# A linear-attention recurrence fused with a gated feed-forward: u read in rows and turned on TensorE, and an order table that reaches one group further

## Chip, core and metric

One core of a Trainium2 chip runs the whole program. The metric is the device time of one execution in microseconds (us). Engines are called as the profile calls them: PE (TensorE), DVE (VectorE), ACT (ScalarE), POOL (GpSimd) and SP (SyncE, which issues almost all DMAs).

## The reference

```python
# r, k, v, w: (4, 8, 768, 48) = batch, heads, sequence, head size; u: (8, 48)
for t in range(S):
    cur = np.einsum('bhd,bhe->bhde', u[None] * kt, vt)
    y[:, :, t] = np.einsum('bhd,bhde->bhe', rt, state + cur)
    state = wt[:, :, :, None] * state + np.einsum('bhd,bhe->bhde', kt, vt)
# x: y as (3072 tokens, 384)
g = x @ w_gate                        # (384, 1536)
silu = g * (1.0 / (1.0 + np.exp(-g)))
out = (silu * (x @ w_val)) @ w_out    # (1536, 384)
```

Everything is float32.

## The kernel before

The sequence is cut into 24 chunks of 128 tokens (6 for each batch). Two heads share a tile, so a chunk has 4 pairs of heads on 112 partitions. One chunk n of the recurrence takes these steps, named as in the kernel:

- loads on SP: `ws` (decays), `kr` (k and r), `vt` (v) and, from chunk 6 on, `nat` (k and r with tokens on partitions);
- DVE: `scan`, `seed`, `scan2` (products of decays), `kq` and `re` (k and r scaled by them, in place), `pred` (one for each head of a pair: keeps the causal part), `sps` and `st` (the state), `ru`, `ruk` and `a0` (the u term from `nat`), and for later chunks `xl`;
- ACT: `whole`, `kn`, `diag`, `vz`, `spb`, `xh`, and `xl` for early chunks;
- PE: `kb` (k turned), `sc` (scores), `dl` (what a chunk adds to the state), `y` (output, already turned for the next matmul), `xm`.

For chunks 0 to 5 the u term comes another way: `prod` (DVE) makes k times r, and `kb` has four matmuls of `prod` with `u_head`, a tile that holds u with head size on partitions, two columns for each pair. `prod` has one buffer (it shares it with `nat`), so `prod:1` must wait until `kb:0` has read `prod:0`. `diag` needs the result through `kn`.

The feed-forward works on groups of 4, 2, 4, 4, 4, 4 and 2 chunks (`GROUPS`), in 12 blocks of 128 hidden columns each. A block f of group g is: `gv:g:f:0` and `gv:g:f:1` (gate and value, 9 matmuls each, on 512 tokens or 256 for a group of two), `silu` (ACT), `sg` (DVE), `hh` (ACT), `hl` (DVE), and `po` (3 matmuls for each chunk of the group). Weights are split in an upper and a lower part (`raw`, `top`, `low`, `shift`, `sign`, `plus`, `upper`, `lower`) while they come in, once, in group 0. The two `gv` results in PSUM have two buffers, so `gv` of the next block waits for `silu` and `sg` of this one. `spin:n` is n matmuls on a constant, for no result.

Two things set the order. The string `ORDER` (line 47) lists steps by name, and on each engine, SP included, the instructions run in that order, each waiting for what it needs. What stands behind the table is written as loops (from line 605): blocks of the remaining groups, with the steps of the remaining chunks (`attention_steps`) strewn between them, and here the framework's scheduler places DVE and ACT work, also among the last steps of the table. `FREE = 2` says that the table holds the blocks of groups 0 and 1; it holds chunks 0 to 9 whole, and the preparation of chunk 10.

`u_head` is filled at lines 182 to 188: a memset on DVE and two DMAs on ACT's queue, each of which reads four rows of 48 numbers and writes them across partitions, one number at a time.

Of the kernel before, what the change touches and what calls it, by code (L numbers as in the profile page):

```python
# [48 lines left out]
scan2:0 kb:0 spin:7 kn:0 re:0 ws:2 diag:0:0 prod:1 sc:0 spin:19 scan:1 diag:0:1 pred:0:0 whole:1
seed:1 kq:1 top:0 pred:0:1 scan2:1 dl:0 spin:6 low:0 st:0 ws:3 shift:0 kb:1 vz:1 vz:0 re:1 y:0  # L50
kn:1 sign:0 diag:1:0 sc:1 spin:9 kr:4 prod:2 vt:2 diag:1:1 plus:0 xh:0 pred:1:0 upper:0 raw:2 xm:0
spin:9 pred:1:1 xl:0 lower:0 top:1 dl:1 spin:16 sps:1 low:1 shift:1 st:1 sign:1 spb:1 y:1 spin:5
scan:2 plus:1 xh:1 vt:3 whole:2 kr:5 xm:1 spin:10 xl:1 seed:2 upper:1 raw:3 kq:2 sps:2 kb:2 spin:5
scan2:2 spb:2 vz:2 kn:2 lower:1 ws:4 diag:2:0 dl:2 spin:11 st:2 diag:2:1 re:2 prod:3 sc:2 spin:13
top:2 scan:3 vz:3 pred:2:0 whole:3 low:2 kq:3 seed:3 kb:3 pred:2:1 scan2:3 y:2 spin:5 kn:3
diag:3:0 shift:2 ws:5 re:3 vt:4 diag:3:1 sps:3 sc:3 sign:2 xh:2 low:3 xm:2 spin:9 pred:3:1
pred:3:0 xl:2 plus:2 spb:3 dl:3 top:3 y:3 spin:7 prod:4 raw:4 upper:2 scan:4 xh:3 vt:5 st:3 vz:4
xm:3 spin:5 whole:4 lower:2 xl:3 gv:0:0:0 kq:4 shift:3 seed:4 sign:3 kb:4 silu:0:0 gv:0:0:1 top:4
scan2:4 kn:4 plus:3 ws:6 vz:5 diag:4:0 gv:0:1:0 re:4 raw:5 upper:3 sg:0:0 scan:5 sc:4 hh:0:0
diag:4:1 lower:3 gv:0:1:1 whole:5 low:4 seed:5 shift:4 hl:0:0 sign:4 po:0:0 silu:0:1 top:5 sg:0:1  # L60
plus:4 low:5 gv:0:2:0 hh:0:1 sps:4 raw:6 pred:4:0 upper:4 pred:4:1 gv:0:2:1 spb:4 hl:0:1 lower:4
silu:0:2 dl:4 gv:0:3:0 sg:0:2 st:4 hh:0:2 shift:5 hl:0:2 gv:0:3:1 sign:5 top:6 low:6 sps:5 plus:5
po:0:1 silu:0:3 prod:5 upper:5 raw:7 sg:0:3 po:0:2 kq:5 hh:0:3 lower:5 hl:0:3 kb:5 gv:0:4:0
shift:6 kn:5 nat:6 diag:5:0 scan2:5 sign:6 po:0:3 ws:7 top:7 re:5 low:7 plus:6 y:4 silu:0:4 scan:6
upper:6 raw:8 gv:0:4:1 ru:6 diag:5:1 vt:6 seed:6 lower:6 kr:6 whole:6 spb:5 gv:0:5:0 xh:4 ruk:6
sg:0:4 a0:6 hh:0:4 shift:7 xm:4 nat:7 diag:6:0 gv:0:5:1 hl:0:4 sign:7 top:8 po:0:4 vz:6 plus:7
silu:0:5 xl:4 low:8 kq:6 raw:9 sc:5 sg:0:5 upper:7 scan2:6 gv:0:6:0 hh:0:5 lower:7 ws:8 gv:0:6:1
hl:0:5 shift:8 silu:0:6 re:6 sign:8 po:0:5 top:9 sg:0:6 low:9 plus:8 gv:0:7:0 hh:0:6 scan:7
upper:8 raw:10 gv:0:7:1 hl:0:6 whole:7 seed:7 silu:0:7 lower:8 po:0:6 pred:5:1 sg:0:7 shift:9
hh:0:7 pred:5:0 kb:6 gv:0:8:0 top:10 sign:9 kn:6 hl:0:7 low:10 y:5 plus:9 silu:0:8 ru:7 raw:11  # L70
upper:9 po:0:7 ruk:7 a0:7 diag:6:1 kr:7 lower:9 nat:8 vt:7 gv:0:8:1 diag:7:0 shift:10 xh:5 sign:10
xm:5 gv:0:9:0 xl:5 sg:0:8 plus:10 top:11 sc:6 hh:0:8 upper:10 kq:7 gv:0:9:1 pred:6:1 low:11 hl:0:8
pred:6:0 silu:0:9 po:0:8 lower:10 vz:7 sg:0:9 gv:0:10:0 shift:11 hh:0:9 ru:8 sign:11 gv:0:10:1
ruk:8 plus:11 dl:6 a0:8 upper:11 y:6 st:6 nat:9 hl:0:9 kb:7 lower:11 silu:0:10 vt:8 po:0:9 kr:8
diag:8:0 sg:0:10 kn:7 sps:7 scan2:7 hh:0:10 gv:0:11:0 diag:7:1 ru:9 ws:9 hl:0:10 vz:8 spb:7
gv:0:11:1 ruk:9 silu:0:11 re:7 a0:9 scan:8 nat:10 po:0:10 xh:6 sg:0:11 whole:8 seed:8 hh:0:11 kq:8
xm:6 hl:0:11 gv:1:0:0 xl:6 scan2:8 po:0:11 silu:1:0 ru:10 ws:10 re:8 ruk:10 sc:7 scan:9 ob:0:1
ob:0:0 out:0:1 gv:1:0:1 out:0:0 seed:9 whole:9 pred:7:1 pred:7:0 gv:1:1:0 sg:1:0 dl:7 hh:1:0
ob:0:3 y:7 hl:1:0 st:7 out:0:3 silu:1:1 sps:8 ob:0:2 out:0:2 po:1:0 diag:8:1 vt:9 kr:9 kb:8
diag:9:0 gv:1:1:1 a0:10 nat:11 gv:1:2:0 spb:8 sg:1:1 kn:8 hh:1:1 gv:1:2:1 vz:9 hl:1:1 xh:7  # L80
silu:1:2 po:1:1 sg:1:2 hh:1:2 kq:9 xm:7 gv:1:3:0 hl:1:2 xl:7 scan2:9 po:1:2 silu:1:3 re:9 ws:11
sc:8 scan:10 gv:1:3:1 pred:8:1 whole:10 seed:10 gv:1:4:0 pred:8:0 sg:1:3 dl:8 hh:1:3 y:8 hl:1:3
st:8 silu:1:4 sps:9 kb:9 diag:9:1 vt:10 po:1:3 kr:10 kn:9 gv:1:4:1 xh:8 spb:9 xm:8 gv:1:5:0 sg:1:4
xl:8 hh:1:4 vz:10 sc:9 hl:1:4 silu:1:5 gv:1:5:1 kq:10 pred:9:0 gv:1:6:0 sg:1:5 scan2:10 hh:1:5
dl:9 gv:1:6:1 st:9 check:10 re:10 po:1:4 hl:1:5 pred:9:1 silu:1:6 po:1:5 ws:12 sg:1:6 hh:1:6
gv:1:7:0 hl:1:6 gv:1:7:1 silu:1:7 y:9 sg:1:7 hh:1:7 hl:1:7 gv:1:8:0 xh:9 kr:11 vt:11 gv:1:8:1
silu:1:8 gv:1:9:0 sg:1:8 po:1:6 po:1:7 hh:1:8 hl:1:8 gv:1:9:1 silu:1:9 gv:1:10:0 sg:1:9 hh:1:9
gv:1:10:1 hl:1:9 silu:1:10 gv:1:11:0 sg:1:10 gv:1:11:1 po:1:8 po:1:9 hh:1:10 hl:1:10 xm:9
# [670 lines left out]
```

## Time and profile before

| | us |
|---|---|
| runs of this kernel, median of 3 (lowest, highest) | 593.75 (593.44, 595.37) |
| the profiled execution's own time | 594.61 |
| its span, first to last instruction | 592.9 |
| PE busy | 572.4 |
| DVE busy | 325.4 |
| ACT busy | 282.8 |

The difference of 1.7 between the profiled execution's time and its span lies ahead of the first instruction and behind the last. A busy PE in this profile is one with a matmul under way, and since matmuls overlap, their durations add up to more than the time. What a step costs PE is therefore read from where the next step begins. A wait is given as the idle time of an engine, with the engine or the DMA that ended it; the chain of waits follows the work that ended last back through the program.

### The profile page before, as it was taken

What the parts mean: (1) busy time and instruction counts of PE and PEld (TensorE: products, weight loads), DVE (VectorE), ACT (ScalarE), POOL (GpSimd) and SP (SyncE); (2) the same over time, 40 slices, a digit from 0 to 9 for tenths busy, and PEclk for the clock granted to TensorE, in tenths of its full rate; (3) what the DMA queues carried; (4) which work ended last, traced back from release to release, by engine and by line L of the source; (5) the groups of instructions that cost most, each with busy time, mean ns of one, the idle gap of its engine ahead of it and who ended that gap; (6) DMA issues with size and microseconds to landing.
All of it is one profiled execution on the core that took longest, in us unless ns stands there. A gap on an engine that the chain in (4) does not pass through costs nothing.

```text
span 592.9 us, 12527 instructions
## 1 busy us (share of the span) xinstructions
PE 572.4 (97%) x5330; PEld 495.1 (83%) x5330; DVE 325.4 (55%) x511; ACT 282.8 (48%) x638; POOL 1.8 (0%) x11
## 2 busy tenths in 40 slices
...
GB/s 252 258 173 184 113 242 180 153 87 128 101 68 65 33 83 72 50 54 72 85 104 103 50 104 116 101 57 72 17 45 47 54 1 1 1 1 1 53 1 33
DMA packets 22734, 50.63 MB, mean 85 GB/s; under 512 B 2992, under 2 KB 9264, under 8 KB 22672
## 3 DMA queue, kind: packets, MB, share of 16 engines
...
q10 hardware_dynamic: 416, 0.00, 0.0%
...
## 4 chain that ended last, share of the span: by engine, by line
PE 87%; ACT 5%; DMA 4%; DVE 2%; issue 1%; ACTq 0%; DVEq 0%
PE gv L522 49%; PE po L556 25%; PE y L422 5%; PE sc L366 4%; PE idle L589 1%; PE dl L390 1%; DMA kr<-in_kr_dram 1%; DMA nat<-in_nat_dram 1%; PE kb L342 1%; DMA u_head<-in_u_rows_dram 1%; ACT at L327 1%; PE kb L344 1%; ACT kn L352 1%; ACT w_h L234 0%; ACT raw L213 0%
## 5 line engine op out<-in xcount | busy, mean ns | idle before, releaser
L522 PE MATMUL gv<-xh,w_h 128*128 128x512 f32 (+1 forms) x504 | 184.1, 365 | 2.4 <-ACT sg L531 2.3
L522 PE MATMUL gv<-xl,w_h 128*128 128x512 f32 (+1 forms) x504 | 182.1, 361 | 0.0
L522 PE MATMUL gv<-xh,w_l 128*128 128x512 f32 (+1 forms) x504 | 181.8, 361 | 0.0
L534 DVE TENSOR_TENSOR sg<-sg,gv 128x512 f32<-128x512 f32 (+1 forms) x84 | 50.9, 606 | 145.2 <-PE gv L522 135.0
L522 PEld LDWEIGHTS gv<-xh,w_h 128*128 128x128 f32 x504 | 94.7, 188 | 18.6 <-ACT sg L531 3.3
L522 PEld LDWEIGHTS gv<-xl,w_h 128*128 128x128 f32 x504 | 94.8, 188 | 14.9
L522 PEld LDWEIGHTS gv<-xh,w_l 128*128 128x128 f32 x504 | 94.8, 188 | 12.8
L556 PE MATMUL po<-w_h,hh 128*128 128x384 f32 x288 | 100.7, 350 | 0.4 <-ACT hh L539 0.4
L556 PE MATMUL po<-w_h,hl 128*128 128x384 f32 x288 | 97.2, 338 | 1.7 <-DVE hl L544 1.7
L556 PE MATMUL po<-w_l,hh 128*128 128x384 f32 x288 | 96.9, 336 | 0.0
L539 ACT ACTIVATE hh<-sg 128x512 fp32r<-128x512 f32 (+1 forms) x84 | 47.8, 569 | 98.0 <-DVE sg L534 93.5
L531 ACT ACTIVATE sg<-gv 128x512 f32<-128x512 f32 (+1 forms) x84 | 44.6, 531 | 96.0 <-PE gv L522 89.4
L544 DVE TENSOR_TENSOR hl<-sg,hh 128x512 fp32r<-128x512 f32 (+1 forms) x84 | 51.6, 614 | 46.1 <-ACT hh L539 45.7
L556 PEld LDWEIGHTS po<-w_h,hh 128*128 128x128 f32 x288 | 54.0, 187 | 7.0 <-issue 4.3
L556 PEld LDWEIGHTS po<-w_h,hl 128*128 128x128 f32 x288 | 54.1, 188 | 3.6 <-DVE hl L544 2.6
L556 PEld LDWEIGHTS po<-w_l,hh 128*128 128x128 f32 x288 | 54.0, 188 | 0.0
L327 ACT ACTIVATE at<-ident,a 128x128 f32<-128x128 f32 x144 | 45.5, 390 | 1.1 <-PE y L422 0.9
L371 DVE COPY_PREDICATED at<-mask,sc 128x512 f32<-128x512 uint32 x48 | 33.0, 729 | 6.4 <-PE sc L366 6.3
L303 ACT ACTIVATE ws<-ws 112x517 f32<-112x517 f32 x24 | 15.3, 639 | 43.3 <-DVE et L292 28.1
L275 DVE TENSOR_TENSOR_SCAN qt<-ws,d1q 112x516 f32<-112x516 f32 x24 | 29.5, 1227 | 1.5 <-DMA ws<-in_wt_dram 1.4
L287 DVE TENSOR_TENSOR kr<-kr,qt 112x512 f32<-112x512 f32 x24 | 16.5, 687 | 24.6 <-DMA kr<-in_kr_dram 24.6
L366 PE MATMUL sc<-kr 48*64 48x128 f32 x768 | 28.6, 282 | 1.2 <-ACT kn L352 1.2
...
## 6 DMA issues: line engine op xcount, KB each, us to landing
kr<-in_kr_dram SPq DMA_DIRECT2D x24, 448.0 KB, 4.1
...
vt<-in_vn_dram SPq DMA_DIRECT2D x24, 192.0 KB, 3.7
out_dram<-ob SPq DMA_DIRECT2D x24, 192.0 KB, 1.9
u_bc<-in_u_dram SPq DMA_DIRECT2D x1, 192.0 KB, 6.7
```

What stands on the lines that cost most here:

```text
L275: keep(nc.vector.tensor_tensor_scan(_flat(qts[n])[:, ::-1], wss[n][:, 1:][:, ::-1], _flat(d1q)[:, ::-1], 0.0, ALU.mult, ALU.add))
L287: keep(nc.vector.tensor_tensor(k, k, qts[n][:, :, 1:], ALU.mult))
L327: keep(nc.scalar.activation(a[:, p, :], ident, AF.Copy, scale=d))
L366: pin(nc.tensor.matmul(scs[n][j][ms, p, :], krs[n][o, 0, p, ms], krs[n][o, 1, p, :], start=True, stop=True,))
L371: keep(nc.vector.copy_predicated(ats[n, j], mask4, scs[n][j]))
L422: pin(nc.tensor.matmul(ys[n][32 * q : 32 * q + 32, b // 4, :], lhs, rhs, start=start[q] == i, stop=stop[q] == i,))
L522: pin(nc.tensor.matmul(ps, a[:, f, j, q * P : (q + 1) * P], x[:, q, :], start=m == 0, stop=m == 3 * NK - 1,))
L531: keep(nc.scalar.activation(sgs[g, f], ps, AF.Silu))
L534: keep(nc.vector.tensor_tensor(sgs[g, f], sgs[g, f], gvs.pop((g, f, 1)), ALU.mult))
L539: keep(nc.scalar.activation(hhs[g, f], t, AF.Copy))
L544: keep(nc.vector.tensor_tensor(hls[g, f], t, hhs[g, f].bitcast(F32), ALU.subtract))
L556: pin(nc.tensor.matmul(pos[g][j], a[:, ts], x[:, f, 2, :], start=f == 0 and i == 0, stop=f == NF - 1 and i == 2,))
```

## The change

The DMAs of u now read rows into a tile `u_two` (8 partitions, one for each head; heads of the second half of a pair 64 columns on). A new step `uh` turns it on PE into PSUM, and ACT copies it to `u_head`, which now holds its two columns per pair with a stride. `FREE` becomes 3: the table has the blocks of group 2 as well, chunks 0 to 13 whole and the preparation of chunk 14; all of the table is written anew.

```diff
-FREE = 2
+FREE = 3
...
-spin:22 ws:0 kr:0 ws:1 kr:1 raw:0 vt:0 scan:0 vt:1 kr:2 ub:0 seed:0 whole:0 raw:1 prod:0 kq:0 kr:3
+spin:21 uh ws:0 kr:0 ws:1 kr:1 raw:0 vt:0 scan:0 vt:1 kr:2 ub:0 seed:0 whole:0 raw:1 prod:0 kq:0
...
+    u_two = mp.tile([H, PR], F32, tag="ob", name="u_two", bufs=2)
+    u_head = cpool.tile([PR, 2, NPR], F32, tag="u_head", name="u_head")
+    nc.vector.memset(u_two, 0.0)
+    for j in range(2):
+        nc.scalar.dma_start(u_two[NPR * j : NPR * j + NPR, 64 * j : 64 * j + D], u_rows[j:H:2, :])
+
     warm = cpool.tile([1, 1], F32, tag="warm", name="warm")
...
-    u_head = cpool.tile([PR, NPR, 2], F32, tag="u_head", name="u_head")
-    nc.vector.memset(u_head, 0.0)
-    for j in range(2):
-        nc.scalar.dma_start(
-            u_head[64 * j : 64 * j + D, :, j], u_rows[j:H:2, :].rearrange("p d -> d p"),
-            allow_slow_non_contiguous=True,
-        )
...
+    def uh():
+        turned = psA.tile([PR, 2, NPR], F32, tag="pa", name="u_turned")
+        pin(nc.tensor.transpose(_flat(turned), u_two, ident[:H, :H]))
+        keep(nc.scalar.activation(u_head, turned, AF.Copy))
...
-                    kbs[n][:, p, PR : PR + 2], prods[n][:, p, :], u_head[:, p, :], start=True, stop=True,
+                    kbs[n][:, p, PR : PR + 2], prods[n][:, p, :], u_head[:, :, p], start=True, stop=True,
```

The first place is PE's order at the start, the last spin ahead of `kb:0` and what follows. Before:

```order
L589 LDWEIGHTS mask
L589 MATMUL idle<-mask 128x256
L342 MATMUL kb_168<-ident,kr_138 128x112
L344 MATMUL kb_168<-u_head,prod_162 128x2
L342 MATMUL kb_168<-ident,kr_138 128x112
```

With the change:

```order
L608 LDWEIGHTS mask
L608 MATMUL idle<-mask 128x256
L323 MATMUL u_turned<-ident,u_two 112x8
L361 MATMUL kb_171<-ident,kr_141 128x112
L363 MATMUL kb_171<-u_head,prod_165 128x2
```

One matmul has come in ahead of `kb:0`, and DVE's first 23 instructions are the same but for the memset.

The second place is DVE's order in group 1, where `nat_11` is the tile of `nat:11`, `kr_9` that of `kr:9`, and `sg_1_2` that of block 2. Before:

```order
L534 TENSOR_TENSOR sg_1_1_1823<-sg_1_1_1823,gv_1_1_1_1856 128x256
L544 TENSOR_TENSOR hl_1_1_1898<-sg_1_1_1823,hh_1_1_1885 128x256
L312 TENSOR_TENSOR nat_11_1868<-nat_11_1868,u_bc_106 128x384
L534 TENSOR_TENSOR sg_1_2_1901<-sg_1_2_1901,gv_1_2_1_1887 128x256
L287 TENSOR_TENSOR kr_9_1844<-kr_9_1844,qt_9_1735 112x512
L315 TENSOR_TENSOR nat_11_1868<-nat_11_1868 128x384
L544 TENSOR_TENSOR hl_1_2_1924<-sg_1_2_1901,hh_1_2_1910 128x256
```

With the change:

```order
L553 TENSOR_TENSOR sg_1_1_1827<-sg_1_1_1827,gv_1_1_1_1851 128x256
L563 TENSOR_TENSOR hl_1_1_1896<-sg_1_1_1827,hh_1_1_1883 128x256
L553 TENSOR_TENSOR sg_1_2_1899<-sg_1_2_1899,gv_1_2_1_1885 128x256
L301 TENSOR_TENSOR kr_9_1844<-kr_9_1844,qt_9_1713 112x512
L306 SCALAR_TENSOR_TENSOR et_9_1929<-ws_9_1516,d1q_84 112x516
L563 TENSOR_TENSOR hl_1_2_1951<-sg_1_2_1899,hh_1_2_1913 128x256
L312 TENSOR_TENSOR kr_9_1844<-kr_9_1844,et_9_1929 112x512
L331 TENSOR_TENSOR nat_11_1868<-nat_11_1868,u_bc_107 128x384
```

The first use of `nat:11` has moved behind `sg` and `hl` of block 2, `kq:9`, `scan2:9` and `re:9`.

The third place is DVE's order where the table ends and the scheduler's own work begins; before, this was in group 1 (blocks 7 to 8, chunk 11):

```order
L544 TENSOR_TENSOR hl_1_7_2250<-sg_1_7_2216,hh_1_7_2248 128x256
L319 TENSOR_REDUCE a0_12_2781<-nat_12_2575 128x8
L287 TENSOR_TENSOR kr_11_2263<-kr_11_2263,qt_11_2453 112x512
L292 SCALAR_TENSOR_TENSOR et_11_2481<-ws_11_1938,d1e_87 112x516
L534 TENSOR_TENSOR sg_1_8_2277<-sg_1_8_2277,gv_1_8_1_2267 128x256
```

With the change it is in group 2 (blocks 7 to 8, chunk 15):

```order
L563 TENSOR_TENSOR hl_2_7_3129<-sg_2_7_3105,hh_2_7_3122 128x512
L301 TENSOR_TENSOR kr_15_3124<-kr_15_3124,qt_15_3356 112x512
L338 TENSOR_REDUCE a0_16_3710<-nat_16_3478 128x8
L306 SCALAR_TENSOR_TENSOR et_15_3384<-ws_15_2931,d1e_87 112x516
L465 TENSOR_TENSOR xl_3_2711<-y_13_3074,xh_3_2710 128x3x128
L312 TENSOR_TENSOR kr_15_3124<-kr_15_3124,et_15_3384 112x512
L289 SCALAR_TENSOR_TENSOR qt_16_3541<-ws_16_3107,d1q_84 112x516
L331 TENSOR_TENSOR nat_17_3712<-nat_17_3712,u_bc_107 128x384
L297 RECIPROCAL d1e_87<-qt_16_3541 112x4
L334 TENSOR_TENSOR nat_17_3712<-nat_17_3712 128x384
L553 TENSOR_TENSOR sg_2_8_3164<-sg_2_8_3164,gv_2_8_1_3154 128x512
```

Nine instructions of later chunks now stand in one piece between `hl` of block 7 and `sg` of block 8; in group 1, where they stood in part, they are gone.

## Rows read from the trace of the kernel before

**Rows 1.** The page: busy time of each engine, share of the span, instructions.

```profile
PE 572.4 (97%) x5330; PEld 495.1 (83%) x5330; DVE 325.4 (55%) x511; ACT 282.8 (48%) x638; POOL 1.8 (0%) x11
```

**Rows 2.** Waits of PE: who waited for whom: us in total, times, longest.

```profile
PE kb L344 <- DMA u_head<-in_u_rows_dram: 3.2, 1, 3.2
...
PE sc L366 <- ACT kn L352: 1.2, 3, 0.6
```

**Rows 3.** Stretches: length, busy PE, PEld, DVE, ACT, POOL, clock, DMA share, GB/s.

```profile
10.05:12.20 2.15, 2.12 (x12) 2.15 (x13) 0.00 (x0) 0.00 (x0) 0.00 (x0) 0.50 1.11 351
...
15.60:49.20 33.60, 32.00 (x597) 25.63 (x594) 32.88 (x45) 27.82 (x60) 0.00 (x0) 1.00 0.67 200
49.20:136.40 87.20, 85.99 (x686) 73.44 (x684) 82.00 (x107) 60.13 (x109) 0.00 (x0) 1.00 0.51 161
```

**Rows 4.** Timeline of the start: start, us, engine, what [idle before, releaser].

```profile
2.54 4.01 PE L589 MATMUL idle<-mask 128*128 128x256 bf16 x22 [2.54 <-POOL mask L160]
...
6.59 0.31 PE L342 MATMUL kb<-ident,kr 112*128 112x112 f32 x1
...
7.91 0.69 DVE L298 TENSOR_TENSOR kr<-kr,et 112x512 f32<-112x512 f32 x1
...
10.08 0.56 PE L344 MATMUL kb<-u_head,prod 112*128 112x2 f32 x2 [3.17 <-DMA u_head<-in_u_rows_dram]
...
12.28 0.69 DVE L309 TENSOR_TENSOR prod<-kr 112x512 f32<-112x512 f32 x1 [3.68 <-PE kb L344]
...
15.80 0.74 DVE L371 COPY_PREDICATED at<-mask,sc 128x512 f32<-128x512 uint32 x1 [1.69 <-PE sc L366]
```

**Rows 5.** DMA issues: what, queue, count, size, median us from issue to landing.

```profile
kr<-in_kr_dram SPq DMA_DIRECT2D x24, 448.0 KB, 4.1
...
out_dram<-ob SPq DMA_DIRECT2D x24, 192.0 KB, 1.9
```

**Rows 6.** The two u_head DMAs, then kr:1: issued from, to; us to landing.

```profile
L185 ACTq DMA_DIRECT2D u_head<-in_u_rows_dram x2: 431/444/457, 2.1 to 2.6; - x2
...
DMA to landing us min/median/max: 6.5/6.9/7.4
...
L259 SPq DMA_DIRECT2D kr<-in_kr_dram x1: 427/427/427, 2.2 to 2.2; - x1
...
DMA to landing us min/median/max: 6.6/6.6/6.6
```

**Rows 7.** Stretches of groups 1 and 2: gv (L522), po (L556), then all instructions.

```profile
136.40:192.73 56.33, 28.75 (x217) 26.59 (x218) 1.00 0.30 88
...
136.40:192.73 56.33, 15.55 (x79) 13.34 (x78) 1.00 0.30 88
...
192.73:283.00 90.27, 89.63 (x797) 76.24 (x797) 45.24 (x72) 36.77 (x91) 0.00 (x0) 1.00 0.20 60
```

**Rows 8.** Chain of waits, undisturbed pieces: start, us, engine, line, matmuls.

```profile
106.95 1.67 PE y L422 x56
...
139.76 1.03 PE sc L366 x32
...
498.23 4.12 PE gv L522 x18
...
551.66 1.05 PE po L556 x6
552.71 2.12 PE gv L522 x18
```

**Rows 9.** Timeline of DVE in group 1: its waits for transfers.

```profile
151.14 0.56 DVE L312 TENSOR_TENSOR nat<-nat,u_bc 128x384 f32<-128x384 f32 x1 [1.64 <-DMA nat<-in_nat_dram]
...
165.70 0.56 DVE L312 TENSOR_TENSOR nat<-nat,u_bc 128x384 f32<-128x384 f32 x1 [2.60 <-DMA nat<-in_nat_dram]
...
179.42 0.69 DVE L287 TENSOR_TENSOR kr<-kr,qt 112x512 f32<-112x512 f32 x1 [1.27 <-DMA kr<-in_kr_dram]
```

**Rows 10.** Groups by line: count, then busy us and mean ns of one.

```profile
L275 DVE TENSOR_TENSOR_SCAN qt<-ws,d1q 112x516 f32<-112x516 f32 x24 | 29.5, 1227 | 1.5 <-DMA ws<-in_wt_dram 1.4
```

More of the change, by code (lines that the diff above doesn't have):

```diff
@@ L47 @@
 ORDER = """
-spin:22 ws:0 kr:0 ws:1 kr:1 raw:0 vt:0 scan:0 vt:1 kr:2 ub:0 seed:0 whole:0 raw:1 prod:0 kq:0 kr:3
[L49 to L88, printed above, removed]
@@ L89 @@
-silu:1:11 po:1:10 xl:9 sg:1:11 hh:1:11 hl:1:11
+spin:21 uh ws:0 kr:0 ws:1 kr:1 raw:0 vt:0 scan:0 vt:1 kr:2 ub:0 seed:0 whole:0 raw:1 prod:0 kq:0
+kr:3 scan2:0 kb:0 spin:6 re:0 kn:0 ws:2 diag:0:0 prod:1 sc:0 spin:19 scan:1 diag:0:1 pred:0:0
+whole:1 seed:1 kq:1 top:0 pred:0:1 scan2:1 dl:0 spin:7 low:0 st:0 ws:3 shift:0 kb:1 vz:1 vz:0 re:1
+y:0 sign:0 kn:1 diag:1:0 sc:1 spin:11 vt:2 prod:2 kr:4 diag:1:1 plus:0 xh:0 pred:1:0 raw:2 upper:0
+xm:0 spin:9 pred:1:1 xl:0 sps:1 lower:0 top:1 dl:1 spin:10 spb:1 st:1 shift:1 low:1 y:1 spin:5
@@ new lines @@
+scan:2 sign:1 whole:2 xh:1 vt:3 vz:2 kr:5 xm:1 spin:7 sps:2 xl:1 kq:2 spb:2 plus:1 kb:2 spin:5
+seed:2 kn:2 raw:3 prod:3 upper:1 dl:2 spin:13 scan2:2 diag:2:1 st:2 ws:4 re:2 diag:2:0 lower:1
+sc:2 spin:18 top:2 scan:3 low:2 pred:2:0 kq:3 vz:3 seed:3 whole:3 kb:3 pred:2:1 scan2:3 y:2 spin:4
+kn:3 diag:3:0 shift:2 ws:5 re:3 vt:4 xh:2 sps:3 sc:3 diag:3:1 sign:2 xm:2 spin:8 spb:3 pred:3:0
+xl:2 pred:3:1 top:3 dl:3 plus:2 y:3 spin:12 low:3 st:3 raw:4 scan:4 upper:2 vt:5 prod:4 xh:3
+lower:2 vz:4 xm:3 spin:5 whole:4 xl:3 gv:0:0:0 kq:4 shift:3 seed:4 sign:3 gv:0:0:1 silu:0:0
```

49 lines of the change are left out of this document (48 added, 1 removed).

## Prediction, made before the change was run

> **What bounds the kernel now.** I read the page first: PE is busy for 572.4 us, 97% of the span [rows 1]. So it is PE's own work that sets the time, and a change can gain only where PE does something useless or slow, or waits. The stretches, next, tell where. Up to 49.2 us the four first chunks are worked through and the first block of group 0 has not begun; from 15.6 on DVE is busy for 32.9 of 33.6 us there, so DVE sets the pace of the start [rows 3]. From 49.2 to 136.4 PE has 86.0 of 87.2 and DVE 82.0 [rows 3]: both nearly full. Then the waits of PE name the longest one: `kb:0` for the DMA of u_head, 3.2 us [rows 2]. The timeline shows what it costs behind PE: `kb:0` begins at 6.59, stops for u_head until 10.08, and `prod:1` on DVE, which needs the buffer that `kb:0` reads, starts at 12.28 after 3.68 idle; the first `pred` starts at 15.80 after another 1.69, for `sc:0` [rows 4]. Part of that is the clock: in 10.05 to 12.20 the granted clock was 0.50, the lower of the two levels (1.2 GHz), after PE had stood still for those 3.2 us [rows 2, 3].
>
> The second place is group 1. Undisturbed, nine `gv` matmuls on 256 tokens take 1.06 (2.12 for 18), six `po` matmuls 1.05, `sc` 1.03, `y` 1.67 [rows 8]. The stretch from 136.4 to 192.73 holds 24 `gv` stages (217 matmuls, one of them the next stage's) and 13 times six `po` (79, one over) [rows 7], and three chunks. That is 25.4 + 13.7 + 3 x 2.7 = 47.2; the nine smaller steps of these chunks (`dl`, `kb`, `xm`) I put at a third of `sc` each, an estimate, 3. Of the 56.3 us [rows 7] about 6 are lost. DVE's timeline gives the cause: three times it waited for a transfer, 1.64, 2.60 and 1.27 [rows 9], with `sg` or `hl` of a block queued behind it, and PE waits for those.
>
> **The change, part by part.** I count from the profiled execution, 594.61 us.
>
> (a) u in rows. Taken away is the wait of `kb:0`; added are one matmul (`uh`), an ACT copy of 112x8 and a memset of 8 partitions. In the new order `uh` follows 21 spins, so it can start at about 6.5 (22 of them ended at 6.55 [rows 4]). A matmul of `kb` took 0.31 [rows 4], and I allow 0.3 for the copy and its handover: u_head is there at 7.1, and `kb:0` ends near 8.2 at the full clock. DVE is free at 8.60, when `re:0` ends [rows 4]; but `prod:1` also needs `kr:1`, which was issued at 2.20 and landed 6.6 later, at 8.80 [rows 6]. So `prod:1` starts at 8.85, 3.4 earlier. That landing also covers `uh`: u may land as late as 7.0 at no cost. Then `scan:1` (1.23 [rows 10]) ends at 10.7, with `sc:0` done by 9.9 at the full clock (six spins and `sc` behind `kb:0`) and ACT's `diag` about then, and the first `pred` starts at 10.75 in place of 15.80: 5.0 earlier. DVE sets the pace from there [rows 3] and its next instructions are the same ones, so I take **-5.0**. How long the new DMA takes no row shows. Below it stand 1.9 for the stores, most of them in quiet stretches [rows 5]; above it 6.5 and 7.4 for the old form of the same bytes, and 6.6 for the load issued beside it [rows 6]. Issued at 2.1 and 2.6 like the old ones [rows 6], it has 4.4 us until 7.0. I take 3.5, nearer to the store, as it moves 8 rows where the old form wrote 384 single numbers. Bounds: 0 if it lands like the old one, -5.4 if all idle time of DVE goes.
>
> The Trainium skill, "DMA: Bandwidth & Descriptors", section "Issuing engines are not separate DMA queues", speaks against this: DMAs of all issuing engines share the same 16 DMA engines and interleave, and a second queue saves only issue time. By that the rows of u would land with their neighbour `kr:1`, at 8.8, and the sum would be about 3 us higher. The trace agrees as far as it goes: the old DMAs of u took 6.5 and 7.4, `kr:1` beside them 6.6 [rows 6].
>
> (b) Spins. The table has 160 for 158, but 139 for 136 behind the first stretch; at 0.18 each (4.01 / 22 [rows 4]) that is **+0.5** if none of it hides a wait. Bounds: +1.0, and -1.0 if the spins that are placed anew shorten waits.
>
> (c) Group 0: the same blocks with DVE and PE both nearly full [rows 3]. Both start 5 us earlier together, so nothing is given back: **0**. Bounds: -1.5 and +1.5.
>
> (d) Group 1. In the new order the first use of `nat:11` stands behind five more DVE instructions, that of `nat:12` behind `hl` of two more blocks, and the use of `kr:11` behind the first `gv` stage of group 2. The three waits of 5.5 us together [rows 9] should go. I keep a quarter of the loss, since loads are still asked for 4 to 5 us ahead: **-4.5**. Bounds: -6, all of it; +1, new waits in their place.
>
> (e) The end of the table. What the scheduler puts among the last steps now meets blocks 7 and 8 of group 2. Nine DVE instructions stand there ahead of `sg` of block 8: two scans (1.23 [rows 10]), two of 0.69, four of about 0.56 [rows 9] and a small one, 6.2 in all. They wait for `kr:15`, asked for when `y:13` ends; at 4.1 to land [rows 5], DVE reaches `sg` 10.3 after that and ends it some 0.6 later, at 10.9. PE has two `po` (2.10, twice 1.05) and three `gv` (2.06) until then [rows 8], 10.4. That gives **+0.5**. Bounds: 0 and +1.7.
>
> (f) Group 2. PE waited 1.2 us in all for `kn` at the first `sc` of three groups [rows 2], because the loops turn it with no block between; one of the three goes: **-0.5**. Bounds: -1.5, and +2 if loads of the packed chunks come late.
>
> The sum is -5.0 + 0.5 + 0 - 4.5 + 0.5 - 0.5 = -9.0: 585.6 against the profiled 594.61, and **584.8** against the median of the runs, 593.75.
>
> **Rivals.**
> - Waits of group 1 stay, under other names, and only the start gains: 593.75 - 5.0 + 0.5 = 589.3. For it: loads are still close to their use, and blocks of 256 tokens are short (2.12 and 1.05 [rows 8]). Against: each of the three waits of rows 9 has an instruction behind it that was moved ahead.
> - The start gains little. Either u lands at 8.8, or weights and decays arrive no earlier than before, as the DMA share was 1.11 and 0.67 there [rows 3], and DVE, 5 us ahead, meets them. `prod:1` then starts near 10.3 and the start gives 2: 587.8.
> - Slower: transfers in group 2. The table puts chunks 10 to 13 into blocks 4 to 7, where before they were spread over the group. Eight loads (`kr:12` to `kr:15`, `nat:13` to `nat:16`) have 4 to 5 us of PE's work between issue and use, and DVE waits in order, with `sg` and `hl` behind it. If they landed like `kr:1` (6.6 [rows 6]), each would cost about 2.2, 17 to 18 in all: 602. It decides against the change when they land later than some 5.7 on average. Against: the DMA share in that stretch was 0.20 [rows 7].
> - The change does nothing that can be measured, because DVE and PE meet the next limit each time: 593.
>
> **How the numbers follow.** The forecast has 0.61, the first rival 0.19, the second 0.12, the third 0.04, the last 0.04. About 0.3%, 1.8 us, is what a measurement of this kernel can tell from no change. Faster by more than that are the first three cases, 0.92; the same 0.04; slower 0.04. The range goes from 581.0 (the forecast with (d) whole and a little from (b) and (f)) to 590.0, which takes in both of the milder rivals with about 1 us for (c) and (e).
>
> **What would show it.** Right: no wait of PE for a DMA at the start, the granted clock at full level from 10 to 15.6, `prod:1` at about 8.9, the first `pred` near 10.8 and the first `gv` at 44 to 45 in place of 49.2; group 1's waits for `nat` and `kr` on DVE below 1.5 in sum; the first `gv` of group 2 about 9 us earlier than 192.7. Wrong: `uh` waiting for u beyond 7; DVE idle between 15 and 45; waits for `kr` or `nat` in group 2 above 2 us; or a gain at 49.2 that is gone at 136.

## The result and the profile after

The changed kernel takes 587.59 us (median of 4 runs, 586.02 to 588.45) beside 594.37 for the kernel before on the same chip (4 runs, 593.44 to 595.37): a ratio of 0.9883, 95% interval 0.9852 to 0.9913. It is faster by 6.8 us; the forecast was 9.0. The profiled execution took 586.91, its span is 585.2, 7.7 less than the span before.

Where the 7.7 us come from is read from the first `gv` matmul of each group; the stretches between are lengths in us. All kernels of the study stand here, each with the stretches of its own profiled execution and the median of its runs. One of the six executions behind the last row took 698.82 us at a mean granted clock of 0.753; it is left out of the median there.

| kernel | median | first `gv` of group 0 | group 0 | group 1 | group 2 | from group 3 to the span's end |
|---|---|---|---|---|---|---|
| before | 593.75 | 49.2 | 87.2 | 56.3 | 89.1 | 311.1 |
| changed | 587.59 | 46.6 | 86.9 | 52.9 | 87.6 | 311.2 |
| e1, only u in rows | 590.93 | 46.3 | 87.1 | 56.3 | 89.1 | 311.0 |
| e2, only the table | 589.36 | 49.8 | 86.1 | 52.8 | 87.8 | 311.3 |
| e3, new order, old reach | 592.42 | 48.1 | 86.2 | 54.6 | 92.7 | 311.1 |
| e4, old order, new reach | 598.31 | 46.2 | 87.3 | 52.9 | 96.4 | 313.3 |
| e5, copy of u behind pend | 585.14 | 45.5 | 86.0 | 52.7 | 87.8 | 311.1 |
| e6, u loaded first | 585.22 | 45.7 | 86.3 | 52.7 | 87.8 | 309.7 |
| e7, x tile 3 first | 589.39 | 46.0 | 90.1 | 52.7 | 88.7 | 310.8 |
| e8, e5 with e6 | 585.25 | 44.4 | 86.1 | 52.8 | 89.1 | 310.4 |
| e9, e8 and ACT's order | 584.18 | 43.0 | 86.7 | 52.5 | 88.1 | 310.6 |
| e10, two more spins | 585.92 | 45.7 | 86.4 | 52.9 | 88.4 | 311.0 |
| changed, once more | 587.09 | 46.4 | 87.1 | 53.0 | 87.7 | 311.1 |

So the start gave 2.6, group 0 0.3, group 1 3.4 and group 2 1.4, and hardly anything (0.1) is given back later. The stretches are those of one execution each: the two of the changed kernel differ by up to 0.3 in a stretch, and e3, whose program is the same up to the first `gv`, has that `gv` 1.6 later (why stands under e10). The runs come from several chips, so kernels are compared by their ratios to the kernel before, run beside each on its chip. By these, e5, e6, e8 and e10 (0.9844 to 0.9866) can't be told from the changed kernel (0.9883, and 0.9867 once more): the 95% intervals overlap. What is said of those four below is read from single executions.

The page's first lines and PE's waits of the changed kernel answer to [rows 1, 2]:

```profile
PE 570.4 (97%) x5333; PEld 494.4 (84%) x5333; DVE 325.1 (56%) x511; ACT 283.9 (49%) x639; POOL 1.8 (0%) x11
```

The waits of PE (who waited for whom, us in total, times, longest):

```profile
PE y L454 <- ACT xh L450: 1.5, 2, 1.3
...
PE sc L385 <- ACT kn L371: 0.5, 2, 0.3
```

PE's busy time is 2.0 less; the other 5.7 of the 7.7 were time with no matmul under way (592.9 - 572.4 before, 585.2 - 570.4 now). The 3.2 us of waiting for u have become 0.6, and `sc` waits 0.5 for `kn` where it waited 1.2.

The timeline of the start, which answers to [rows 4]:

```profile
2.54 4.42 PE L608 MATMUL idle<-mask 128*128 128x256 bf16 x21 [2.54 <-POOL mask L176]
...
7.55 0.19 PE L323 MATMUL u_turned<-ident,u_two 8*112 8x8 f32 x1 [0.59 <-DMA u_two<-in_u_rows_dram]
...
7.78 0.18 ACT L324 ACTIVATE u_head<-u_turned 112x8 f32<-112x8 f32 x1 [3.23 <-PE u_turned L323]
7.85 0.20 ACT L294 ACTIVATE pend<-qt 112x4 f32<-112x4 f32 x1
...
8.09 1.23 DVE L306 TENSOR_TENSOR_SCAN et<-ws,d1e 112x516 f32<-112x516 f32 x1 [1.39 <-ACT pend L294]
...
9.96 0.69 DVE L328 TENSOR_TENSOR prod<-kr 112x512 f32<-112x512 f32 x1
```

and, from 9.8 us on:

```profile
10.10 1.99 PE L385 MATMUL sc<-kr 48*64 48x128 f32 x32 [0.17 <-DVE kr L312]
...
12.21 0.73 DVE L390 COPY_PREDICATED at<-mask,sc 128x512 f32<-128x512 uint32 x1 [0.43 <-PE sc L385]
```

The chain of waits names the transfer (start, us, what):

```profile
2.77 4.65 DMA u_two<-in_u_rows_dram
```

The first DMA of u was issued at 2.17, the second at 2.77; it landed 4.65 us later, at 7.42. `kr:1`, issued beside them at 2.20, landed at 7.4 in this execution, 5.2 us after its issue:

```profile
L273 SPq DMA_DIRECT2D kr<-in_kr_dram x1: 436/436/436, 2.2 to 2.2; - x1
...
DMA to landing us min/median/max: 5.2/5.2/5.2
```

`u_turned` waited for u, and then ACT copied u at 7.78, in front of its copy of pend at 7.85. That copy reads the decays' products (`qt`) of chunk 0, whose only buffer the second scan needs: DVE stood still for 1.39 until 8.09. `prod:1` came at 9.96, in place of 12.28, and the first `pred` at 12.21, in place of 15.80.

The stretches (length, busy PE, PEld, DVE, ACT, POOL, clock, DMA share, GB/s) answer to [rows 3, 7]:

```profile
10.00:13.41 3.41, 3.31 (x39) 2.59 (x40) 2.98 (x6) 3.41 (x10) 0.00 (x0) 0.50 1.05 345
...
46.59:133.47 86.88, 86.35 (x687) 73.84 (x684) 83.25 (x108) 59.72 (x108) 0.00 (x0) 1.00 0.48 157
133.47:186.35 52.88, 52.86 (x676) 49.94 (x676) 28.44 (x58) 26.57 (x74) 0.00 (x0) 1.00 0.28 85
```

From 10.00 to 13.41 the granted clock was 0.50, 1.2 GHz; `sc:0` took 1.99 there, and at the full level it takes 1.10 (below). In group 1 PE now has no idle time to speak of: 52.86 of 52.88. DVE had six kinds of waits in that group, and none names a transfer, against the three of [rows 9]; the longest in sum is:

```profile
DVE hl L563 <- ACT hh L558: 8.2, 6, 3.1
```

Of the 3.6 us at the first `pred` only 2.6 were left at the first `gv` (in the second execution of the changed kernel 3.1 and 2.8, so the loss is not the same each time). Between them DVE was nearly full and waited for no transfer; the last place where PE stood still shows in the timeline of ACT and PE:

```profile
42.97 1.39 ACT L232 ACTIVATE raw<-raw 128x1152 int32<-128x1152 uint32 x1
...
44.12 1.28 ACT L248 ACTIVATE w_h<-s 128x1152 fp32r<-128x1152 f32 x1
...
45.17 0.60 ACT L450 ACTIVATE xh<-y 128x384 fp32r<-128x384 f32 x1
...
45.83 0.44 PE L454 MATMUL y<-xh,minus 128*128 128x384 f32 x1 [1.25 <-ACT xh L450]
...
46.59 0.48 PE L541 MATMUL gv<-xh,w_h 128*128 128x512 f32 x1
```

`y:3` ended at 43.15 (its last matmuls ran from 42.66 for 0.49), but its copy `xh:3` stands on ACT behind two steps of weights, `low:3` and `upper:2`, and began at 45.17.

### The profile page after: what moved, and what is told of

Same layout as the page of the kernel before. It is cut to its first block, busy times and chain, and to the rows that moved or that the text cites. A ratio compares the mean times of both kernels' runs of the same rounds, so it can differ in the third digit from the quotient of the medians.

```text
span 585.2 us, 12525 instructions
## 1 busy us (share of the span) xinstructions
PE 570.4 (97%) x5333; PEld 494.4 (84%) x5333; DVE 325.1 (56%) x511; ACT 283.9 (49%) x639; POOL 1.8 (0%) x11
## 4 chain that ended last, share of the span: by engine, by line
PE 83%; ACT 6%; DMA 5%; DVE 4%; issue 1%; SPq 0%; ACTq 0%; DVEq 0%
PE gv L541 46%; PE po L575 24%; PE y L441 5%; PE sc L385 4%; DMA raw<-in_wo_dram 2%; PE idle L608 2%; ACT at L346 1%; PE kb L361 1%; PE dl L409 1%; ACT raw L227 1%; DVE et L306 1%; DMA kr<-in_kr_dram 1%; DMA u_two<-in_u_rows_dram 1%; ACT raw L232 1%; ACT w_h L248 1%
## 5 line engine op out<-in xcount | busy, mean ns | idle before, releaser
L306 DVE TENSOR_TENSOR_SCAN et<-ws,d1e 112x516 f32<-112x516 f32 x24 | 29.4, 1225 | 1.5 <-ACT pend L294 1.4
```

The lines of the kernel that those rows point to most:

```text
L306: keep(nc.vector.tensor_tensor_scan(_flat(ets[n]), wss[n][:, :L], _flat(d1e), 0.0, ALU.mult, ALU.add))
```

## The experiments

My theory after the result: u in rows gives what the start gives, the table what groups 1 and 2 give; u's transfer, ACT's order and the clock ate the rest of the start. The first four kernels take the change apart.

**e1: u in rows alone.** The code of the change with the table of before.

```diff
-FREE = 3
+FREE = 2
-(the new ORDER)
+(the old ORDER, "spin:21 uh" in place of "spin:22")
```

> Only the way u is read is changed (rows and uh, one spin fewer); the order table is the old one, FREE stays 2. Theory: the start gain of the whole change (first gv 2.6 us earlier) is u's alone, so 594.4 - 2.6 = 591.8, first gv at 46.5 to 47, group 1 (first gv of group 1 to first gv of group 2) as long as before, 56.3. Rival: the start gain comes from the new order; then 594 and a first gv at 49.

Measured: 590.93 (590.09 to 592.42), ratio 0.9935 (0.991 to 0.996). The first `gv` came at 46.3, group 1 kept its 56.3, and the waits of DVE in 136 to 195 were still there, 4.2 for `nat` and 1.3 for `kr`:

```profile
DVE nat L314 <- DMA nat<-in_nat_dram: 4.2, 2, 2.3
```

So u in rows gives the gain of the start, and only that.

**e2: the table alone.**

```diff
-spin:21 uh ws:0 kr:0 ...
+spin:22 ws:0 kr:0 ...
```

with u loaded as before, and `FREE = 3`.

> Only the order table is changed (FREE 3, all items of the new one, uh left out, 22 spins); u is read number by number as before. Theory: the wait of kb:0 for u_head comes back, first gv at 49 to 50; group 1 and 2 together as short as in the change (140.5 from first gv of group 1 to that of group 3, against 145.4); so 594.4 - 5 = 589.5. Rival (the start carries more, as orders interact): 592.

Measured: 589.36 (588.87 to 590.7), ratio 0.9912 (0.9891 to 0.9934). The wait for u stays, the first `gv` is at 49.8, and groups 1 and 2 take 140.6 together as in the changed kernel (140.5):

```profile
PE kb L359 <- DMA u_head<-in_u_rows_dram: 2.7, 1, 2.7
```

By the stretches, each half gives its gain where the whole change has it. By the ratios the two gains add up to 1.5%, more than the 1.2% of the whole; the intervals are too wide to say that this means anything. The next two ask what in the table does it: its order, or that it reaches one group further.

**e3: the new order, as far as the old table went.** Of the new table only the items that the old one holds; the scheduler places the rest.

```diff
-FREE = 3
+FREE = 2
...
-kb:9 y:8 hl:1:4 kn:9 po:1:4 diag:9:1 vt:10 kr:10 ...
+(the same items in the same order, without those the old ORDER lacks)
```

> u in rows and the new order, but only those items that the old table had: groups 0 and 1; group 2 is left to the loops (FREE 2). Theory: the uses of nat:11 and nat:12 are moved, so two of the three DVE waits of group 1 go, but the scheduler's nine instructions stand in blocks 7 and 8 of group 1 again and cost 2 to 2.5: 587.6 + 2.3 = 590. Rival: the extension to group 2 alone matters, then 592; second rival: the extension does nothing, then 587.6.

Measured: 592.42 (590.33 to 594.45), ratio 0.9948 (0.993 to 0.9967): no faster than u in rows alone. The waits for transfers came back in group 1 and the start of group 2 although everything in the table stands in its new order (group 1 is 1.7 shorter than before, with the wait for `kr` now behind its end):

```profile
149.69 0.56 DVE L314 TENSOR_TENSOR nat<-nat,u_bc 128x384 f32<-128x384 f32 x1 [2.32 <-DMA nat<-in_nat_dram]
...
167.15 0.56 DVE L314 TENSOR_TENSOR nat<-nat,u_bc 128x384 f32<-128x384 f32 x1 [2.00 <-DMA nat<-in_nat_dram]
...
190.47 0.69 DVE L284 TENSOR_TENSOR kr<-kr,qt 112x512 f32<-112x512 f32 x1 [1.78 <-DMA kr<-in_kr_dram]
```

The profiled execution, 594.45, is the longest of its seven, and its granted clock was 0.50 from 192.85 to 196.26, so the 92.7 of group 2 holds more than the order.

**e4: the old order, with the new reach.** The old table, and behind it, in the new order, the items that only the new one has.

```diff
+FREE = 3
...
-(the new ORDER)
+(spin:21 uh, the old ORDER, then the new ORDER's further items)
```

> u in rows, the old order for groups 0 and 1 and behind it the items that only the new table has (FREE 3). Theory: the waits for nat:11 and nat:12 stay (about 2.5), those at the old table's end go: 594.4 - 2.6 - 2.4 = 589.4. Rival: the new order within groups 0 and 1 is what gives group 1 its gain, then 591.8 as with u alone.

Measured: 598.31 (596.85 to 601.06), ratio 1.0068 (1.0043 to 1.0093). Group 1 took 52.9, as short as in the changed kernel, with the old order. The users of the late tiles now stand behind the last step of group 1. In group 2 DVE waits 3.8 for `nat` and 0.8 for `kr`, and PE lost 6.85 in one piece, waiting for a `silu`:

```profile
189.72 0.56 DVE L330 TENSOR_TENSOR nat<-nat,u_bc 128x384 f32<-128x384 f32 x1 [3.04 <-DMA nat<-in_nat_dram]
```

That is DVE's timeline; PE's is:

```profile
197.61 0.79 PE L540 MATMUL gv<-xh,w_h 128*128 128x512 f32 x1 [6.85 <-ACT sg L549]
```

Part of what group 2 lost is the clock, which fell while PE waited and was still low for 3 us behind the wait (columns as in the stretches above):

```profile
193.76:200.58 6.82, 2.97 (x7) 2.39 (x8) 4.75 (x8) 5.92 (x17) 0.00 (x0) 0.50 0.46 126
```

The waiting steps of group 1 were not steps of the old table. `ru:11`, `ru:12` and `kq:11`, the first users of the three late tiles, aren't in it: the scheduler put them in among the table's last steps, and they waited there with `sg` and `hl` behind them. The table's longer reach takes them out of the scheduler's hands, and so out of group 1. It does not pay by itself: e4 is slower than the kernel before. That the new order keeps the work they belong to from piling up in group 2 (87.6 against 96.4) is a reading of these two kernels, which differ in the whole order.

The next runs are on the start.

**e5: ACT copies u behind pend.**

```diff
 def uh():
-    turned = psA.tile([PR, 2, NPR], F32, tag="pa", name="u_turned")
-    pin(nc.tensor.transpose(_flat(turned), u_two, ident[:H, :H]))
-    keep(nc.scalar.activation(u_head, turned, AF.Copy))
+    xs["u"] = psA.tile([PR, 2, NPR], F32, tag="pa", name="u_turned")
+    pin(nc.tensor.transpose(_flat(xs["u"]), u_two, ident[:H, :H]))
+def uc():
+    keep(nc.scalar.activation(u_head, xs["u"], AF.Copy))
-... seed:0 whole:0 raw:1 ...
+... seed:0 whole:0 uc raw:1 ...
```

> Edit: on ACT the copy of the turned u stands behind the copy of pend instead of ahead of it; PE and DVE keep their order. Theory (the copy of u, which waits for the transfer of u until 7.4 and for PE until 7.7, holds pend and with it the second scan on DVE): the second scan of chunk 0 starts at about 6.7 instead of 8.09, the product of chunk 1 at 8.6 instead of 9.96; the scores of chunk 0 no longer wait for r and start at 9.5 to 10.0 instead of 10.10, the first pred at 11.6 to 12.0 instead of 12.21, the first gate matmul 0 to 0.6 earlier; time -0.6 to 0 against the changed kernel. Rival (PE's spins and the lower clock hold the start, not pend): the second scan starts earlier as well but the first pred stays at 12.2 within 0.1 and the first gate matmul within 0.2.

Measured: 585.14 (584.12 to 588.6), ratio 0.9866 (0.9826 to 0.9907). The timeline of DVE and PE:

```profile
6.66 1.23 DVE L305 TENSOR_TENSOR_SCAN et<-ws,d1e 112x516 f32<-112x516 f32 x1
...
7.72 0.19 PE L322 MATMUL u_turned<-ident,u_two 8*112 8x8 f32 x1 [0.52 <-DMA u_two<-in_u_rows_dram]
...
9.46 0.69 DVE L329 TENSOR_TENSOR prod<-kr 112x512 f32<-112x512 f32 x1 [0.84 <-PE kb L364]
...
10.02 1.10 PE L386 MATMUL sc<-kr 48*64 48x128 f32 x32
...
11.40 0.73 DVE L391 COPY_PREDICATED at<-mask,sc 128x512 f32<-128x512 uint32 x1
```

The second scan starts at 6.66, and the first `pred` at 11.40, 0.2 earlier than the theory's best; the first `gv` is 1.1 earlier, more than it allowed. The median is 2.4 lower, but the ratio, 0.9866, is that of the changed kernel once more (0.9867), so no gain in time is shown. What the theory had not foreseen: the clock read 1.00 from 10.00 to 13.40, so `sc:0` took 1.10; and the product of chunk 1 came at 9.46, not 8.6, because it waited 0.84 for `kb:0`.

**e6: u loaded first.** The block of `u_two` (tile, memset, two DMAs) goes ahead of `ident`, so that the DMAs are ACT's first instructions, issued from 1.08 on instead of 2.17.

> Edit: the zeroing of the u tile is DVE's first instruction and its two DMAs are ACT's first, so they are issued about 1 us earlier. Theory (u is late because of the time from issue to landing, 4.65 us for the second DMA whenever it is issued): u lands at about 6.4 instead of 7.4, PE turns it behind the 21 spins at about 7.0 instead of 7.55, the first kb starts at 7.1 to 7.2 instead of 7.67, the second scan at 7.5 to 7.7 instead of 8.09, the first pred 0.3 to 0.6 earlier, the first gate matmul 0 to 0.6 earlier. Rival (the two small DMAs wait behind the bulk loads of the start, which they share the engines with): u lands at 7.2 to 7.6 as before, and nothing moves.

Measured: 585.22 (583.79 to 585.82), ratio 0.9855 (0.9832 to 0.9878). The theory held up to the second scan; the first `pred` and the first `gv` came 0.9 earlier, more than it allowed. The timeline of PE and DVE:

```profile
7.13 0.23 PE L323 MATMUL u_turned<-ident,u_two 8*112 8x8 f32 x1
...
7.70 1.23 DVE L306 TENSOR_TENSOR_SCAN et<-ws,d1e 112x516 f32<-112x516 f32 x1 [1.05 <-ACT pend L294]
...
9.58 0.68 DVE L328 TENSOR_TENSOR prod<-kr 112x512 f32<-112x512 f32 x1
...
11.32 0.71 DVE L390 COPY_PREDICATED at<-mask,sc 128x512 f32<-128x512 uint32 x1
```

u is there when PE comes to it, right behind the spins: it landed by 7.13 and is no longer waited for. The second scan still waited 1.05 for pend, and `prod:1` follows it and `re:0` on DVE without idle time, so it is pend that holds `prod:1` now: `kb:0`'s last matmul ran from 8.57 for 0.29. The clock was full from 10 here too, and `sc:0` took 1.10.

**e7: the last x tile of group 0 first.**

```diff
-y:3 spin:12 low:3 st:3 raw:4 scan:4 upper:2 vt:5 prod:4 xh:3 lower:2 vz:4 xm:3 spin:5 whole:4 xl:3
+y:3 spin:5 xh:3 xm:3 spin:5 xl:3 low:3 st:3 raw:4 scan:4 upper:2 vt:5 prod:4 lower:2 vz:4 whole:4
```

> Edit: on ACT the two halves of the last x tile of group 0 (xh:3, xl:3) stand directly behind the y matmuls, ahead of low:3 and upper:2; on DVE lower:2 comes behind prod:4. Theory (the last microsecond before the first gate matmul is lost to ACT's order, xh:3 at 45.17 though y:3 ended at 43.15): xh:3 starts at 43.2 to 43.5, the first gate matmul at 44.4 to 45.2 instead of 46.59. If group 0 is bound by PE, the time falls by 1.3 to 2.0; rival: group 0's preparation of the weights on DVE and ACT (low:3, upper:2, lower:2 now later by 1.0 to 1.5) takes it back inside the group as waits of PE, and the first gate matmul of group 1 is at 133.0 to 133.5 as before, time within 0.5.

Measured: 589.39 (588.45 to 589.97), ratio 0.9917 (0.9893 to 0.994), above the changed kernel's 0.9883 (the intervals just overlap) and 0.9867 once more (they don't). The first `gv` came only 0.6 earlier, and group 0 took 90.1 in place of 86.9: the rival, and worse. `upper:2`, now last on ACT, made `lower:2` on DVE wait, and DVE, nearly full in this group, passed it on to PE. DVE's timeline:

```profile
48.39 1.36 DVE L250 TENSOR_TENSOR w_l<-s,w_h 128x1152 fp32r<-128x1152 f32 x1 [2.38 <-ACT w_h L247]
```

and PE's:

```profile
56.06 0.79 PE L540 MATMUL gv<-xh,w_h 128*128 128x512 f32 x1 [2.57 <-DVE sg L552]
```

At the end of that wait the granted clock fell, to 0.50 from 56.00 to 59.41, so the 3.2 us that group 0 lost are the wait and the clock together.

**e8: e5 and e6 together.**

> Edit: the two edits of the start together: u loaded about 1 us earlier, and ACT's copy of the turned u behind pend. Theory (with u early, kb of chunk 0 ends at 8.9 and frees the buffer that the product of chunk 1 waited for until 9.46; with pend early the second scan starts at 6.7): the product of chunk 1 starts at 8.9 to 9.1 (9.46 with the order alone, 9.58 with the load alone), DVE has no idle time over 0.5 from there on, the first pred at 10.9 to 11.1, the first gate matmul at 44.8 to 45.3 (45.5 and 45.7 with one edit alone); time 0.2 to 0.7 below either of them, about 584.7. Rival (the two gains are the same gain, that of the granted clock staying full from 10 on): the first gate matmul at 45.5 as with one edit alone.

Measured: 585.25 (583.86 to 587.34), ratio 0.9851 (0.983 to 0.9872). DVE's timeline at the start:

```profile
8.78 0.68 DVE L329 TENSOR_TENSOR prod<-kr 112x512 f32<-112x512 f32 x1
...
10.52 0.71 DVE L391 COPY_PREDICATED at<-mask,sc 128x512 f32<-128x512 uint32 x1
```

The start went as the theory has it, and a little further: `prod:1` at 8.78, the first `pred` at 10.52, the first `gv` at 44.4. The time, forecast 0.2 to 0.7 lower, did not fall with it. Group 2 took 89.1 in place of 87.8 in e5, where DVE waited 2.3 for one load of `kr` and PE 1.4 for a `silu` (by who waited for whom; that the earlier start brings DVE there ahead of the load is my reading and was not tried). PE's wait in 184 to 274, which e5 does not have:

```profile
PE gv L542 <- ACT sg L551: 1.4, 1, 1.4
```

**e9: e8, and ACT's order before the first `gv`.** As in e7, but `upper:2` keeps its place and `low:3` goes into the 2 us in which ACT waits for the first `silu`.

```diff
-y:3 spin:12 low:3 st:3 raw:4 scan:4 upper:2 vt:5 prod:4 xh:3 lower:2 vz:4 xm:3 spin:5 whole:4 xl:3
+y:3 spin:5 st:3 raw:4 xh:3 scan:4 upper:2 xm:3 spin:10 vt:5 prod:4 xl:3 lower:2 vz:4 low:3 whole:4
```

> Edit: on top of the two edits of the start, ACT's order before the first gate matmul is xh:3, upper:2, xl:3, low:3 (low:3 goes into the 2 us that ACT waits for the first silu; upper:2 and lower:2 keep their places against DVE). Theory: xh:3 starts as soon as y:3 ends, the first gate matmul 0.7 to 1.2 earlier than with the two edits of the start alone, DVE's weight steps are no later, PE waits in group 0 stay under 1, and the time falls by 0.5 to 1.2 more, to about 583.8. Rival (DVE and ACT are the bound of group 0 whatever the start): group 0 gets longer by what its first matmul came earlier, the first gate matmul of group 1 is where it is without this edit within 0.3.

Measured: 584.18 (582.73 to 585.66), ratio 0.9831 (0.9815 to 0.9848). It has the lowest median of the study, 1.1 under e8 (their intervals overlap) and 2.9 under the changed kernel beside it (587.09; the intervals, 0.9815 to 0.9848 and 0.9843 to 0.9891, only touch). The timeline before the first `gv`:

```profile
41.16 0.49 ACT L451 ACTIVATE xh<-y 128x384 fp32r<-128x384 f32 x1 [0.17 <-PE y L442]
...
43.01 0.47 PE L542 MATMUL gv<-xh,w_h 128*128 128x512 f32 x1
```

`xh:3` starts with the end of `y:3`, the first `gv` at 43.0, 1.4 before e8. Group 0 took 0.6 more than in e8, so 0.8 of the 1.4 is left at the first `gv` of group 1 (129.7 against 130.5): mostly the theory.

**e10: two more spins ahead of u.** `spin:23 uh` in place of `spin:21 uh`.

> Edit: the changed kernel with 23 idle matmuls ahead of the turning of u instead of 21, so that PE stands idle 0.1 to 0.2 there instead of 0.59. Theory (the idle time of PE ahead of u is what the clock falls for from 10.0 to 13.4): the granted clock stays full over 10 to 13.4, the scores of chunk 0 take 1.1 instead of 1.9, the first pred is at 11.7 to 11.9 instead of 12.21 and the first gate matmul 0.3 to 0.8 earlier than 46.6. Rival (that idle time has no part in it; with the copy of u behind pend the idle time was 0.52 and the clock stayed full): the clock falls to half at about 10 as before, and the first pred stays at 12.1 to 12.4.

Measured: 585.92 (583.29 to 586.52), ratio 0.9844 (0.982 to 0.9868). The timeline:

```profile
7.78 0.19 PE L323 MATMUL u_turned<-ident,u_two 8*112 8x8 f32 x1 [0.24 <-DMA u_two<-in_u_rows_dram]
...
11.94 0.71 DVE L390 COPY_PREDICATED at<-mask,sc 128x512 f32<-128x512 uint32 x1
```

The stretch, as above:

```profile
10.00:13.40 3.40, 3.23 (x53) 2.64 (x51) 3.40 (x7) 3.37 (x11) 0.00 (x0) 1.00 1.07 301
```

PE waited 0.24 for u, the clock stayed full and the first `pred` came at 11.94, though the scan and pend were held by u as before (second scan at 8.31). The theory held in this execution (the first `gv`, at 45.7, is 0.9 earlier, a little more than it had). But the idle time ahead of u is not all: e3 and e7 have the start of the changed kernel, `u_turned` waited only 0.40 and 0.23 there, and `sc:0` took 1.99 in both, as at the lower level. In e7:

```profile
11.35 1.99 PE L384 MATMUL sc<-kr 48*64 48x128 f32 x32
```

The clock's row reads full there all the same:

```profile
10.00:13.40 3.40, 3.40 (x40) 2.41 (x41) 1.83 (x2) 3.21 (x11) 0.00 (x0) 1.00 1.07 325
```

The matmuls of `kb:0` took 0.43 there in place of 0.29 as well, from 7.59 on. So in these two executions `kb:0` and `sc:0` ran as at the lower level, whatever the row says, and e3 has its first `pred` at 13.63 and its first `gv` at 48.1 with a start that is the changed kernel's.

**The changed kernel once more,** with the last three on one chip:

> The changed kernel once more, on the chip of the variants of its start. Every theory expects 587.6 within 1.0, the granted clock at half from about 10.0 to 13.4, the first pred at 12.2 and the first gate matmul at 46.6; should the clock stay full here, the fall differs from one execution to the next, and the start of the profiled run is not that of all runs.

Measured: 587.09 (584.09 to 588.32), ratio 0.9867 (0.9843 to 0.9891). The clock fell again, by the timeline and the stretch:

```profile
7.99 0.19 PE L323 MATMUL u_turned<-ident,u_two 8*112 8x8 f32 x1 [1.06 <-DMA u_two<-in_u_rows_dram]
...
10.57 1.99 PE L385 MATMUL sc<-kr 48*64 48x128 f32 x32
...
12.69 0.73 DVE L390 COPY_PREDICATED at<-mask,sc 128x512 f32<-128x512 uint32 x1 [0.46 <-PE sc L385]
```

followed by

```profile
10.00:13.40 3.40, 3.40 (x41) 2.41 (x39) 2.94 (x5) 3.37 (x11) 0.00 (x0) 0.51 1.05 325
```

u landed 0.4 later than in the first profile, and the first `pred`, at 12.69, is 0.5 later than forecast; the first `gv`, at 46.4, isn't. Of the seven executions of the changed kernel that are not profiled here, the mean granted clock over the whole span is on record: 0.993 in one, 0.996 to 0.998 in six. No trace of the study in which the clock's row falls near 10 has a mean above 0.995, so in those six the row did not show this fall. What their starts were like instead, full or as in e7, is not on record; nor were they faster (584.09 to 588.45, against 586.91 and 587.09 for the two profiled). The start of the profiled executions is not that of all.

## Why the prediction was right, and where its size came out wrong

The sign, the range and the two places were right: the time lies 2.8 above the forecast, and by the profiled executions the gain is 7.7 of 9.0. The start fell short by 1.9 (-4.5 forecast with the spins of (b), -2.6 measured at the first `gv`), and groups 1 and 2 gave 0.4 more than their three terms. Two of my own signs of being wrong came: `uh` waited for u beyond 7, until 7.55, and the waits for `kr` and `nat` in group 2 are above 2.

**(a), the start.** The step was "I take -5.0", with (b) -4.5; measured are 3.6 at the first `pred` and 2.6 at the first `gv`. Four readings in it failed.
- "I take 3.5" for the transfer: it took 4.65, and 4.81 to 5.09 in e1, e5, e10 and the changed kernel once more. The load beside it (6.6 [rows 6]) was nearer than the stores (1.9). The Trainium skill's rule that DMAs of all issuing engines run on the same 16 DMA engines and interleave ("DMA: Bandwidth & Descriptors", section "Issuing engines are not separate DMA queues") pointed the right way: u landed with its neighbour `kr:1`, 7.42 and 7.4. That both would land at 8.8 was my reading of the old trace. In the changed kernel once more u landed at 7.86 and `kr:1` 6.6 us after 2.21, at 8.8, so landing together is not what every execution shows.
- "It can start at about 6.5": the 21 spins took 4.42 in place of 4.01 for 22, so PE was free at 6.96. In the other traces with 21 spins they took 4.14 to 4.66, and in e6, with u early, `uh` started at 7.13.
- "u may land as late as 7.0 at no cost": I had looked at DVE and PE, and not at what stands behind the new copy on ACT. Pend does, and the second scan needs its buffer. In e6 u is there in time, and DVE still waited 1.05 for pend; with e5 it did not.
- The full clock from 10 on. It fell at about 10.0 in the changed kernel, both times it was profiled, and in e1, and at 9.4 in e4; in e3 and e7 `sc:0` ran at the lower level too. It is not the price of every execution, as the mean clocks above show.

With u early and pend free of it, and the clock full (e8), the chain that I had worked out is what the trace shows: `prod:1` 8.85 forecast, 8.78 measured; first `pred` 10.75 and 10.52; first `gv` 44 to 45 and 44.4.

**(b)** was not separated from (a); in e10 two more spins, put where PE waited for u, cost nothing.

**(c), group 0: 0.** It took 0.3 less. Right: both engines nearly full, and nothing given back.

**(d), (e) and (f), groups 1 and 2: -4.5, +0.5 and -0.5.** Measured: -3.4 in group 1, -1.4 in group 2, together -4.9 for -4.5. The three waits went. But the reason was half wrong: "the first use of `nat:11` stands behind five more DVE instructions" is true of the program, but the new order of the old steps isn't what moved it. By e4 group 1 loses its waits with the old order too, and by e3 two of them are back with the new one (2.32 and 2.00): what counts is that the table ends one group later and so holds these users itself, where the scheduler had put them into group 1. The cost of that, (e), I looked for at the end of group 2 as +0.5. PE did not stand still there (it was busy all of 250 to 262, where `hl` of block 7 ends at 249.0 and `sg` of block 8 starts at 255.45), and the group got shorter; DVE's waits for `kr` and `nat` in it fell, as the waits of DVE in that group show, first of the kernel before:

```profile
DVE kr L287 <- DMA kr<-in_kr_dram: 6.6, 4, 2.5
...
DVE nat L312 <- DMA nat<-in_nat_dram: 2.1, 1, 2.1
```

then of the changed one:

```profile
DVE kr L301 <- DMA kr<-in_kr_dram: 2.5, 2, 1.7
...
DVE nat L331 <- DMA nat<-in_nat_dram: 0.6, 1, 0.6
```

The 3.1 us that are left are over what my mark for "wrong" allowed (2 in group 2); the mark was too strict, as the group is 1.4 shorter. (f) is right: `sc` waits 0.5 for `kn` in place of 1.2 [rows 2].

**The rivals.** The second (the start gains 2) describes the start best, at 2.6, but by neither of its ways: u landed with `kr:1` in the profiled execution, but at 7.4 and not at 8.8, and from the first `pred` to the first `gv` DVE waited for no transfer. The first fell: group 1 lost its waits. The slower one, transfers of group 2, did not come: its loads were waited for less than before. Something like it is seen in e4, where the same steps stand at a worse place and the time is 598.3, though DVE's waits for transfers in group 2 there (4.6) are below those of the kernel before (8.7).

Open: what decides whether the clock is full when `sc:0` runs. The idle time of PE ahead of u, 0.52 in e5 and 0.59 in the changed kernel, can hardly be all of it, as e3 and e7 ran `sc:0` at the lower level with less. Open too is how much of what e5 and e6 show at the start is the clock and how much the order, since in both the clock was full. The price of the clock is not read from e10 either: its first `pred` is 0.3 and its first `gv` 0.9 ahead of the changed kernel's, but against the second execution of that kernel it is 0.75 and 0.7.
